# Reordering the head of a fused attention and two-layer kernel: first slot's Relu deferred, x turned earlier, x scaled by chunk

## The chip, the cores and the metric

The kernel runs on one core of a Trainium2 chip. The metric is the device time in microseconds. A core has five engines with a queue each: TensorE (PE, matrix products), VectorE (DVE), ScalarE (ACT), GpSimd (POOL) and SyncE (SP, which here issues DMA transfers).

## The reference

```
kv  = einsum('bhsd,bhse->bhde', k, v)          # B=8, H=8, S=576, D=64
o   = einsum('bhsd,bhde->bhse', q, kv)
rms = sqrt(mean(o*o, axis=-1) + 1e-6)
x   = (o / rms * g_norm), heads side by side    # 4608 x 512
h   = x @ w_in                                  # w_in 512 x 2048
g   = s * relu(h)**2 + b
out = g @ w_out                                 # w_out 2048 x 512
```

The two weights arrive as 64-bit floats; q, k, v and g_norm as 32-bit floats.

## The kernel before

**Tiling.** The 4608 rows of x are worked in 36 chunks of 128 rows, four chunks to a unit, nine units. For each chunk `attention` (or, for later units, `attention_of_two`) turns q (`turn`, `take`), multiplies it by the block-diagonal k-v product (`product`), squares and sums the rows (`square`: an ACT square and a DVE row sum), takes the root (`root`, ACT), normalises (`norm`, DVE) and turns the result so that x's features lie on partitions (`turn_x`). Turned x of a unit is one tile `xT` of 4 feature parts by 512 columns, 128 columns a chunk. Each feature part has a column of g_norm (`g_col`) that it is multiplied with.

**How x is turned and scaled in the first unit.** Chunks 0 and 1 are turned by four PE transposes each (L487); the results are scaled by g_col while they leave PSUM, chunk 0 on ACT (L490), chunk 1 on DVE (L494). Chunks 2 and 3 are turned by one DVE transpose each (L499), and once both are there `scale_x` (L507 to L510) multiplies both on ACT, in place, in four instructions of 128x256.

**The weights.** A weight tile of 1 MB is loaded by SP into one of three buffers (`w_raw`, L187) and made into 32-bit floats in four steps: `hi` (ACT, L225), `lo` (ACT, L230), `shift` (DVE, L235) and `plus` (DVE, L245). `plus` also issues the next load, into the buffer that it has just freed (`send_w`, L1246). Tiles 0 and 1, the two halves of the first two blocks of w_in, are each converted in two halves, so that the first products can begin earlier; tile 0 becomes `wa` of step 0, tile 1 `wb` of step 0. Tiles 2 to 7 are the rest of w_in, 8 to 15 are w_out.

**The first unit.** Products of the first layer are 16 slots (`mm1_plain`, L669). A slot is `block`: eight matmuls over the four feature parts (16 records in the profile) into a PSUM bank, then Relu on ACT (L682) and a square on DVE (L683). Slot 0 multiplies chunks 0 and 1 by `wa` of step 0, slot 1 the same chunks by `wb`, slot 2 chunks 2 and 3 by `wa`, slot 3 these by `wb`, and slots 4 to 15 repeat it for the next three steps. Even slots use the two x banks by turns, odd slots the two y banks. `first_unit` (L1381) puts the conversion of one tile behind most slots.

After the slots comes the second layer of the unit (`mm2`). The bias is part of it: DVE sums the rows of w_out into `b_row` (`column_sums`, L307), `bias_row` (L353) makes `b_sq` (L355) and PE multiplies the two into `b_ps`; it is called from `with_bias` (L986) after the fifth step of the second layer. Later units multiply with fewer products by sums and differences of quarters; the change does not touch them.

**Order.** The order of work on each engine is that of the program text: the kernel is scheduled by hand. The head, L1296 to L1344, is a list of calls; an instruction that waits holds everything behind it on its engine. In the head the order on ACT after chunk 0's scaling is: second half of tile 0, Relu of slot 0, square of chunk 2, first half of tile 1, square of chunk 3, second half of tile 1, both roots, the scaling of chunks 2 and 3, Relu of slot 1, tile 2.

Of the kernel before, what the change touches and what calls it, by code (L numbers as in the profile page):

```python
# [11 lines left out]
AF = mybir.ActivationFunctionType  # L12
# [4 lines left out]
def kernel(  # L17
# [39 lines left out]
    nc = tc.nc  # L57
# [8 lines left out]
    KC = DM // P  # L66
# [23 lines left out]
    def matmul(o, lhsT, rhs, start, stop):  # L90
        nc.tensor.matmul(o, lhsT=lhsT, rhs=rhs, start=start, stop=stop, skip_group_check=True)  # L91
# [246 lines left out]
    g_col = const.tile([P, KC], FP32, name="g_col")  # L338
# [63 lines left out]
    def half_of(name, c):  # L402

        if c % 2 == 0:
            two_of[name] = attp.tile([P, 2 * DM], FP32, name=name, tag=name)
        t = two_of[name]
        if name == "qT":
            return t.rearrange("p (a x) -> p a x", a=NP)[:, :, c % 2 * P : c % 2 * P + P]
        return t[:, c % 2 * DM : c % 2 * DM + DM].rearrange("p (h d) -> p h d", h=H)

    def small(name, n, i=""):
        return attp.tile([P, n], FP32, name=name, tag=f"{name}{i}")

    def attention(c):

        st = {}  # L420

        def turn():
            st["qT"] = half_of("qT", c)
            if c % 2 == 0:
                ps = ps_a.tile([P, NP, P], FP32, name="qT_ps", tag="x")
            else:
                tag, bufs = ("y", 2) if c == 1 else ("z", 1)
                ps = bank_of("q", tag, bufs).rearrange("p b (m n) -> p (b m) n", m=2)
            for p in range(NP):
                nc.tensor.transpose(ps[:, p, :], q_in[c][:, 2 * p : 2 * p + 2, :], ident)  # L430
            st["q_ps"] = ps

        def take():
            if c % 2 == 0:
                nc.vector.tensor_copy(out=st["qT"], in_=st["q_ps"])  # L435
            else:
                nc.scalar.copy(st["qT"], st["q_ps"])

        def product():
            ps = bank_of("att", "xy"[c % 2]).rearrange("p b (m n) -> p (b m) n", m=2)  # L440
            if c < 2:
                for p in range(NP):
                    matmul(ps[:, p, :], st["qT"][:, p, :], bd_kv[0][:, p, :], True, True)
            for w in range(4 if c >= 2 else 0):
                for p in range(NP):
                    nc.tensor.matmul(
                        ps[32 * p : 32 * p + 32, w, :],
                        lhsT=st["qT"][:, p, 32 * w : 32 * w + 32],
                        rhs=bd_kv[0][:, p, :],
                        start=True,  # L450
                        stop=True,
                    )
            st["x"] = ps.rearrange("p c (l d) -> p (c l) d", l=2)

        def square():
            st["xn"] = half_of("xn", c)
            nc.scalar.activation(st["xn"], st["x"], AF.Square)
            st["ss"] = small("ss", H, c % 2)
            nc.vector.reduce_sum(st["ss"], st["xn"], axis=mybir.AxisListType.X)  # L459

        def root():
            st["rms"] = small("rms", H, c % 2)
            nc.scalar.activation(st["rms"], st["ss"], AF.Sqrt, bias=eps_col, scale=1.0 / D)

        def norm():
            inv = small("inv", H, c % 2)
            nc.vector.reciprocal(inv, st["rms"])
            shape = (P, H, KC, D // KC)
            nc.vector.tensor_tensor(
                out=st["xn"].rearrange("p h d -> p (h d)").rearrange(  # L470
                    "p (c h e) -> p h c e", c=KC, h=H
                ),
                in0=st["x"].rearrange("p h (c e) -> p h c e", c=KC),
                in1=inv.unsqueeze(2).unsqueeze(3).to_broadcast(shape),
                op=ALU.mult,
            )

        def turn_x():
            u, j = divmod(c, 4)
            if j == 0:  # L480
                xT[u] = xp.tile([P, KC, 2 * TB], FP32, name="xT", tag="xT")
            to = xT[u][:, :, j * P : j * P + P]
            if c < 2:
                ps = ps_t.tile([P, KC, P], FP32, name="xT_ps", tag="t")
                xn = st["xn"].rearrange("p h d -> p (h d)")
                for i in range(KC):
                    nc.tensor.transpose(ps[:, i, :], xn[:, i * P : i * P + P], ident)  # L487
                for i in range(KC):
                    if c == 0:
                        nc.scalar.activation(  # L490
                            to[:, i], ps[:, i], AF.Copy, scale=g_col[:, i : i + 1]
                        )
                    else:
                        nc.vector.tensor_scalar(  # L494
                            out=to[:, i], in0=ps[:, i], scalar1=g_col[:, i : i + 1],
                            scalar2=None, op0=ALU.mult,
                        )
                return
            nc.vector.transpose(  # L499
                out=to, in_=st["xn"].rearrange("p h d -> p (h d)").rearrange("p (c x) -> p c x", c=KC)  # L500
            )
            if j % 2 == 1:
                scale_x(u, j - 1)

        return turn, take, product, square, root, norm, turn_x

    def scale_x(u, j):  # L507
        to = xT[u][:, :, j * P : j * P + 2 * P]
        for i in range(KC):
            nc.scalar.activation(to[:, i], to[:, i], AF.Copy, scale=g_col[:, i : i + 1])  # L510
# [134 lines left out]
    def bank_of(key, tag, bufs=2):  # L645
        bank[key] = ps_f.tile([P, 2, TB], FP32, name=f"{tag}_ps", tag=tag, bufs=bufs)
        return bank[key]
# [12 lines left out]
    def g_tile(name, s):  # L660
        if s % 2 == 0:
            g_pair[name, s // 2] = gp.tile([P, 2, 2, TB], FP32, name=name, tag=name)
        ga[name, s] = g_pair[name, s // 2][:, s % 2]
        return ga[name, s]

    def g_s1(s):
        add(ga["s1", s], ga["a21", s], ga["a22", s])

    def mm1_plain(s):  # L669


        def block(lower, half, name, tag):
            ps = bank_of("c", tag)
            w = (wb if lower else wa)[s]
            for c in range(KC):
                for b in range(2):
                    matmul(
                        ps[:, b, :], w[:, c, b], xT[0][:, c, half * TB : half * TB + TB],
                        b == 0 and c == 0, c == KC - 1,
                    )  # L680
            t = g_tile(name, s)
            nc.scalar.activation(t, ps, AF.Relu)  # L682
            nc.vector.tensor_mul(t, t, t)  # L683

        def c22():
            block(1, 1, "a22", "y")
            g_tile("s1", s)
            g_s1(s)

        return [  # L690
            lambda: block(0, 0, "a11", "x"),
            lambda: block(1, 0, "a12", "y"),
            lambda: block(0, 1, "a21", "x"),
            c22,
        ]

# [562 lines left out]
    def hi(n, h=None):  # L1259
        fold_hi(blocks[n], h)  # L1260

    def lo(n, h=None):
        round_lo(blocks[n], h)

    def shift(n, h=None):
        shift_hi(blocks[n], place(n), h)

    def plus(n, h=None):
        add_lo(blocks[n], place(n), h)
        if h != 0:  # L1270
            send_w()
# [17 lines left out]
    turn, take, product, square, root, norm, turn_x = zip(*(attention(c) for c in range(4)))  # L1289
# [3 lines left out]


    slots0 = [slot for s in range(NS) for slot in mm1_plain(s)]
    turn[0]()  # L1296
    turn[1]()
# [12 lines left out]
    norm[1]()  # L1310
    take[3]()
    hi(0, 0)
    product[2]()
    lo(0, 0)
    shift(0, 0)
    turn_x[0]()
    plus(0, 0)
    product[3]()
    hi(0, 1)
    turn_x[1]()  # L1320
    lo(0, 1)
    shift(0, 1)
    plus(0, 1)
    slots0[0]()
    square[2]()
    hi(1, 0)
    lo(1, 0)
    shift(1, 0)
    plus(1, 0)
    square[3]()  # L1330
    hi(1, 1)
    lo(1, 1)
    shift(1, 1)
    plus(1, 1)
    root[2]()
    norm[2]()
    turn_x[2]()
    root[3]()
    norm[3]()
    turn_x[3]()  # L1340
    slots0[1]()
    for step in (hi, lo, shift, plus):
        step(2)
# [37 lines left out]
    def first_unit():  # L1381
        for n, slot in enumerate(slots0):
            if n > 1:
                slot()
            if n in tile_at:
                for step in (hi, lo, shift, plus):
                    step(tile_at[n])
            if n in more_at:
                more(more_at[n])
# [166 lines left out]
```

## Time and profile before

| | |
|---|---|
| time, median of 3 | 926.41 us (925.38 to 927.22) |
| span of the profiled execution | 924.5 us |
| PE busy | 911.0 us, 99% |
| PE weight load busy | 827.1 us, 89% |
| DVE busy | 678.8 us, 73% |
| ACT busy | 209.2 us, 23% |
| GpSimd busy | 220.2 us, 24% |
| mean granted PE clock | 0.996 |
| DMA | 167.70 MB, mean 181 GB/s |

A line of the order of time gives start, duration, engine, line of the kernel, operation, output and input, shapes and count; in brackets the idle time of the engine just before, and what ended it. A line of the stretches gives the stretch, its length, and for PE, PE weight load, DVE, ACT and GpSimd the busy time and the number of instructions; then the granted clock, the DMA share and GB/s. `L91` is the helper through which nearly all matmuls go, so the names of the tiles (x_ps, y_ps, b_ps) tell products apart.

The waits of the first 80 us that are longest for PE, ACT and DVE, once the k-v product is made:

| who waited | for | us |
|---|---|---|
| DVE a L683 | ACT a L682 | 5.2 in 2, longest 2.7 |
| ACT a L682 | PE x_ps L91 | 4.9 in 3, longest 3.7 |
| ACT xT L510 | DVE xT L499 | 3.8 |
| PE y_ps L91 | DVE wb L245 | 3.3 |
| PE x_ps L446 | DVE qT L435 | 2.0 |

### The profile page before, as it was taken

How to read it: one execution, taken by the hardware profiler on the slowest of the kernel's cores; microseconds unless marked ns; L12 is line 12 of the kernel's file. 1: busy time of each engine (PE TensorE's matmuls, PEld its weight loads, DVE VectorE, ACT ScalarE, POOL GpSimd, SP SyncE). 2: the span in 40 equal slices, each digit the busy share in tenths (PEclk: the TensorE clock that was granted, in tenths of full speed). 3: DMA queues.
4: the chain of work that ended last, by engine and by line, in shares of the span. 5: the costliest groups of instructions: out<-in, count | busy, mean ns of one | idle time of the engine just before them, and what ended most of it. 6: DMA issues, size and time to landing. Idle time of an engine off the chain costs nothing.

```text
span 924.5 us, 18300 instructions
## 1 busy us (share of the span) xinstructions
PE 911.0 (99%) x7272; PEld 827.1 (89%) x7272; DVE 678.8 (73%) x1149; ACT 209.2 (23%) x382; POOL 220.2 (24%) x412
## 2 busy tenths in 40 slices
PE   7899999999999999999999999999999999999998
PEld 7688888888888998899889988999889988998898
DVE  2679869587667975887678867786678768864685
ACT  2666122310124002310232013301340033002200
POOL 2000005203623232630264034603330200020000
PEclk9899999999999999999999999999999999999999
DMA  9486957429931894179425954387418900890085
GB/s 270 136 300 234 282 145 222 112 68 325 333 105 35 262 335 126 26 220 308 146 81 157 296 180 115 96 295 247 116 42 278 296 12 12 257 310 26 12 251 183
DMA packets 113605, 167.70 MB, mean 181 GB/s; under 512 B 28400, under 2 KB 45552, under 8 KB 113520
## 3 DMA queue, kind: packets, MB, share of 16 engines
q1 hardware_dynamic: 95504, 141.98, 49.0%
q0 software_dynamic: 14560, 22.31, 8.3%
q10 hardware_dynamic: 3456, 2.23, 0.9%
q8 instruction: 58, 0.95, 0.4%
q14 instruction: 27, 0.22, 0.1%
HBM read 142.35 MB, written 24.12 MB: 180 GB/s over the span
## 4 chain that ended last, share of the span: by engine, by line
PE 97%; DVE 1%; DMA 1%; issue 0%; SPq 0%; ACT 0%; DVEq 0%
PE x_ps L91 51%; PE y_ps L91 29%; PE z_ps L91 11%; PE kv_ps L380 2%; PE y_ps L559 2%; DMA kv_sb<-in_v_dram 1%; PE qT_ps L548 0%; SPq L107 0%; DVE o L858 0%; DVE ss L459 0%; DVE sub L253 0%; DVE qT L435 0%; DVE xn L592 0%; DVE a L253 0%; PE xT_ps L487 0%
## 5 line engine op out<-in xcount | busy, mean ns | idle before, releaser
L1376 POOL DMA_DIRECT2D q_sb<-in_q_dram x256 | 143.7, 569 | 150.4 <-issue 120.0
L703 ACT COPY r<-x_ps 128x512 f32<-128x512 f32 x96 | 55.9, 583 | 453.8 <-PE x_ps L91 424.0
L967 POOL DMA_DIRECT2D out_dram<-o x110 | 54.8, 505 | 406.3 <-DVE o L858 277.7
L91 PE MATMUL x_ps<-w_sb,sub 128*128 128x128 f32 x1176 | 149.3, 276 | 0.7 <-DVE r L858 0.7
L91 PEld LDWEIGHTS x_ps<-w_sb,sub 128*128 128x128 f32 x1176 | 139.7, 192 | 1.5 <-DVE r L858 0.9
L91 PE MATMUL x_ps<-xs,ws 128*128 128x256 f32 x512 | 122.3, 382 | 0.0
L91 PE MATMUL y_ps<-xs,wb 128*128 128x256 f32 x512 | 121.8, 380 | 0.2 <-issue 0.2
L91 PEld LDWEIGHTS x_ps<-xs,ws 128*128 128x128 f32 x512 | 96.2, 190 | 16.5 <-issue 3.8
L91 PEld LDWEIGHTS y_ps<-xs,wb 128*128 128x128 f32 x512 | 96.7, 190 | 14.2 <-issue 0.6
L250 DVE TENSOR_TENSOR a<-y_ps,r 128x512 f32<-128x512 f32 x64 | 44.1, 689 | 83.6 <-ACT r L703 73.3
L91 PE MATMUL x_ps<-xT,wa 128*128 128x256 f32 x384 | 89.6, 380 | 0.5 <-DVE xT L494 0.5
L91 PEld LDWEIGHTS x_ps<-xT,wa 128*128 128x128 f32 x384 | 72.3, 190 | 10.5 <-ACT w_raw L225 0.7
L91 PE MATMUL x_ps<-w_sb,a 128*128 128x128 f32 (+1 forms) x432 | 64.9, 298 | 0.0
L91 PE MATMUL y_ps<-w_sb,a 128*128 128x128 f32 (+1 forms) x416 | 62.1, 295 | 0.0
L91 PEld LDWEIGHTS x_ps<-w_sb,a 128*128 128x128 f32 x432 | 59.0, 191 | 3.2 <-issue 0.4
L91 PE MATMUL x_ps<-xT,ws 128*128 128x256 f32 x256 | 61.2, 382 | 0.0
L91 PE MATMUL z_ps<-xT,wa 128*128 128x256 f32 x256 | 60.5, 379 | 0.0
L658 DVE SCALAR_TENSOR_TENSOR a<-a 128x512 f32<-128x512 f32 x82 | 56.7, 692 | 2.8
L91 PEld LDWEIGHTS y_ps<-w_sb,a 128*128 128x128 f32 x416 | 56.1, 192 | 2.1
L91 PEld LDWEIGHTS z_ps<-xT,wa 128*128 128x128 f32 x256 | 48.6, 190 | 6.6
L91 PEld LDWEIGHTS x_ps<-xT,ws 128*128 128x128 f32 x256 | 48.1, 190 | 6.5
L858 DVE SCALAR_TENSOR_TENSOR r<-x_ps,s_col,o 128x256 f32<-128x256 f32 (+1 forms) x84 | 34.7, 413 | 25.7 <-PE x_ps L91 24.1
(157 smaller groups left out, 1268.8 us busy)
## 6 DMA issues: line engine op xcount, KB each, us to landing
w_sb<-w SPq DMA_DIRECT2D x343, 256.0 KB, 4.7
w_raw<-in_moe_w_in_dram SPq DMA_DIRECT2D x8, 1024.0 KB, 7.7
w_raw<-in_moe_w_out_dram SPq DMA_DIRECT2D x8, 1024.0 KB, 5.2
w_sb<-w SPq DMA_DIRECT2D x14, 512.0 KB, 9.0
w<-sub POOLq DMA_DIRECT2D x28, 256.0 KB, 6.3
w_sb<-in_k_dram SPq DMA_DIRECT2D x24, 288.0 KB, 5.1
w_sb<-in_v_dram SPq DMA_DIRECT2D x24, 288.0 KB, 5.1
out_dram<-o POOLq DMA_DIRECT2D x92, 64.0 KB, 3.6
```

Of the source, the lines that this page charges most:

```text
L91: nc.tensor.matmul(o, lhsT=lhsT, rhs=rhs, start=start, stop=stop, skip_group_check=True)
L250: nc.vector.tensor_tensor(out=o, in0=a, in1=b, op=ALU.add)
L380: nc.tensor.matmul(ps[r][(r ^ l) * HB : (r ^ l) * HB + HB, i, :], lhsT=kv[l][0][rows, j, :], rhs=kv[l][1][rows, j, :], start=(j == 0), sto ...
L559: nc.tensor.matmul(ps[l][32 * p : 32 * p + 32, r, lo:hi], lhsT=bd_kv[b % 2][rows, p, at : at + 32], rhs=st["qT"][rows, p, lo:hi], start=Tr ...
L658: nc.vector.scalar_tensor_tensor(t, t, 0.0, t, ALU.max, ALU.mult)
L703: nc.scalar.copy(st[name], src)
L858: nc.vector.scalar_tensor_tensor(o, ps, s_col, other, ALU.mult, ALU.add)
L967: queues[s % 2].dma_start(out=view[b, jj, :, cols], in_=st[name, j][s * w : s * w + w, cols])
L1376: load()
```

## The change

Three things are done to the head, for the same end: to let the first slots of PE follow each other with less waiting.

- `block` no longer issues Relu and square itself but returns them as a function. For slot 0 that function is called at the end of the head, after the second weight tile's conversion and the work on chunks 2 and 3; everywhere else it is called at once.
- Chunks 0 and 1 are turned ahead of the q products of chunks 2 and 3 (`turn_x[0]` before `product[2]`, `turn_x[1]` before `product[3]`), and the squares, roots and norms of chunks 2 and 3 are moved between the steps of tile 1's conversion.
- Chunks 2 and 3 are scaled each by itself, as soon as it is turned: in eight ACT instructions of 128x128 instead of four of 128x256. Later units still use `scale_x`.

```diff
--- before.py
+++ after.py
@@ -499,8 +499,8 @@
             nc.vector.transpose(
                 out=to, in_=st["xn"].rearrange("p h d -> p (h d)").rearrange("p (c x) -> p c x", c=KC)
             )
-            if j % 2 == 1:
-                scale_x(u, j - 1)
+            for i in range(KC):
+                nc.scalar.activation(to[:, i], to[:, i], AF.Copy, scale=g_col[:, i : i + 1])
 
         return turn, take, product, square, root, norm, turn_x
 
@@ -678,19 +678,22 @@
                         ps[:, b, :], w[:, c, b], xT[0][:, c, half * TB : half * TB + TB],
                         b == 0 and c == 0, c == KC - 1,
                     )
-            t = g_tile(name, s)
-            nc.scalar.activation(t, ps, AF.Relu)
-            nc.vector.tensor_mul(t, t, t)
+            def out_of():
+                t = g_tile(name, s)
+                nc.scalar.activation(t, ps, AF.Relu)
+                nc.vector.tensor_mul(t, t, t)
+
+            return out_of
 
         def c22():
-            block(1, 1, "a22", "y")
+            block(1, 1, "a22", "y")()
             g_tile("s1", s)
             g_s1(s)
 
         return [
             lambda: block(0, 0, "a11", "x"),
-            lambda: block(1, 0, "a12", "y"),
-            lambda: block(0, 1, "a21", "x"),
+            lambda: block(1, 0, "a12", "y")(),
+            lambda: block(0, 1, "a21", "x")(),
             c22,
         ]
 
@@ -1310,34 +1313,35 @@
     norm[1]()
     take[3]()
     hi(0, 0)
+    lo(0, 0)
+    turn_x[0]()
     product[2]()
-    lo(0, 0)
     shift(0, 0)
-    turn_x[0]()
     plus(0, 0)
+    turn_x[1]()
     product[3]()
     hi(0, 1)
-    turn_x[1]()
     lo(0, 1)
     shift(0, 1)
     plus(0, 1)
-    slots0[0]()
+    out_of_first = slots0[0]()
     square[2]()
+    square[3]()
     hi(1, 0)
     lo(1, 0)
     shift(1, 0)
+    root[2]()
+    root[3]()
     plus(1, 0)
-    square[3]()
+    norm[2]()
     hi(1, 1)
     lo(1, 1)
     shift(1, 1)
+    turn_x[2]()
     plus(1, 1)
-    root[2]()
-    norm[2]()
-    turn_x[2]()
-    root[3]()
     norm[3]()
     turn_x[3]()
+    out_of_first()
     slots0[1]()
     for step in (hi, lo, shift, plus):
         step(2)
@@ -1381,7 +1385,9 @@
     def first_unit():
         for n, slot in enumerate(slots0):
             if n > 1:
-                slot()
+                out_of = slot()
+                if out_of:
+                    out_of()
             if n in tile_at:
                 for step in (hi, lo, shift, plus):
                     step(tile_at[n])
```

## The prediction

> **What bounds the kernel now.** I read the 40 slices first, for where TensorE (PE) is not saturated.
>
> ```profile
> ## 2 busy tenths in 40 slices
> PE   7899999999999999999999999999999999999998
> DVE  2679869587667975887678867786678768864685
> PEclk9899999999999999999999999999999999999999
> ```
>
> PE is under 90% only in the first two slices (46 us) and the last; the second also has a granted clock of 0.8. So only the head can give time, or something that begins in the head and pushes on. I then read that head by the waits, by stretches of 2 us, and in order of time. The stretches (PE, weight load, VectorE (DVE), ScalarE (ACT), GpSimd; then clock, DMA share, GB/s):
>
> ```profile
> 28.00:30.00 2.00, 0.38 (x2) 0.00 (x0) 0.96 (x2) 1.59 (x4) 0.00 (x0) 1.00 0.89 234
> 30.00:32.00 2.00, 0.36 (x1) 0.39 (x2) 1.86 (x4) 2.00 (x5) 0.00 (x0) 0.67 0.70 271
> 32.00:34.00 2.00, 2.00 (x6) 1.53 (x6) 1.83 (x5) 0.58 (x3) 0.00 (x0) 0.50 0.00 0
> 36.00:38.00 2.00, 2.00 (x7) 1.62 (x6) 0.39 (x1) 1.58 (x4) 0.00 (x0) 0.62 0.95 347
> ```
>
> PE pauses from 28.4 to 31.64 and then runs at half clock; from 0.67 and 0.62 in the border stretches, half clock lasts from 30.7 to 37.5. The order of time says why it pauses:
>
> ```profile
> 24.54 3.84 PE L91 MATMUL x_ps<-xT,wa 128*128 128x256 f32 x16 [0.54 <-DVE xT L494]
> 28.41 0.60 ACT L682 ACTIVATE a<-x_ps 128x512 f32<-128x512 f32 x1 [3.74 <-PE x_ps L91]
> 31.64 6.58 PE L91 MATMUL y_ps<-xT,wb 128*128 128x256 f32 x16 [3.26 <-DVE wb L245]
> 36.42 1.70 ACT L510 ACTIVATE xT<-xT,g_col 128x256 f32<-128x256 f32 x4 [3.85 <-DVE xT L499]
> 38.06 3.62 PE L91 MATMUL x_ps<-xT,wa 128*128 128x256 f32 x16
> ```
>
> Call a group of 16 records of line 91 a slot: slot 0 at 24.54, slot 1 at 31.64, slot 2 at 38.06. ACT stands 3.74 us at slot 0's Relu, with the next weight tile's folding and the squares of chunks 2 and 3 queued behind it; so slot 1 waits for its weights. Slot 2 takes chunks 2 and 3 of x, whose scaling ACT begins only at 36.42. From 38.06 on slots follow at 3.45 us.
>
> A second thing nearly binds, 60 us later:
>
> ```profile
> 63.65 1.14 ACT L225 ACTIVATE w_raw<-w_raw 128x1024 f32<-128x1024 f32 x1 [1.83 <-DMA w_raw<-in_moe_w_out_dram]
> 64.82 0.69 DVE L235 TENSOR_SCALAR w_up<-w_raw 128x1024 uint32<-128x1024 uint32 x1 [0.90 <-ACT w_raw L225]
> 103.30 0.28 DVE L355 TENSOR_SCALAR b_sq<-b_sq,b_col 128x128 f32<-128x128 f32 x1
> 103.67 1.09 PE L91 MATMUL b_ps<-b_row,b_sq 128*128 128x512 f32 x2
> ```
>
> After the 0.38 us at 65.89 the order of time shows no DVE wait until 105.42: DVE is full from 64.82 to 103.58, and PE's bias product at 103.67 starts 0.09 us after it. The DVE chain has no slack to give PE, and it starts from a load that ACT had waited for.
>
> **What the Trainium skill says.** "TensorE: Matmul & The Clock Gate", Part 1: after about 3.4 us of idling, watched in windows of 3,413 ns that run free of the kernel, the array drops to half clock and needs a busy window to return. The trace agrees: 30.7 to 37.5 is 6.8 us, two windows, after one (27.3 to 30.7) with 1.1 us of work. The same page, "Architectural detail": ACT and DVE queues are strict FIFO. Agrees: the fold at 29.38 stood behind the Relu. "ScalarE: Activation LUTs", "What ACT_TABLE_LOAD costs": 186 ns + 0.833 ns an element, 93 ns for a pointer operand, 93 ns overlap with the next. For the 128x256 scale that is 492 ns; the trace has 1.70 us for four, 0.49 each with a 0.40 step.
>
> **The change, part by part.** I place each instruction with the steps of the trace: ACT 128x512 0.55 (weights) or 0.48 (square, Relu); DVE 0.42 for a half-tile shift, 0.69 for 128x512, about 0.08 of overlap between independent operations, none between dependent ones.
>
> *Turning chunk 0 and 1 first.* norm[0] ends at 20.08, so chunk 0's transposes run 20.15 to 20.8, in PE time that was idle (2.04 us before the product at 20.74); product[2] keeps its place (qT is ready at 20.69), chunk 1's transposes run at 21.8 instead of 23.34, product[3] at 22.35. ACT scales chunk 0 from 21.0 (was 22.44); DVE scales chunk 1 from 22.6 (was 24.04), right after the first half tile's add. The second half's shift and add then end at 24.9 (were 26.3). Slot 0 begins when product[3] leaves PE, 23.4, and ends at 26.9: 1.2 earlier. Nothing is added; four transposes change places.
>
> *Relu and square of slot 0 deferred.* ACT goes straight on: squares of chunk 2 at 23.1 and 3 at 23.6, then the fold of weight tile 1 at 24.1 (was 29.38). That tile was issued at 13.7 and landed 10.3 us later, at 24.0, so this just fits. DVE: two row sums 24.8 to 26.1, shift 26.0, add 26.6 to 27.3 (was 31.50); slot 1 starts at 27.35. Then norm[2] to 28.1, second shift, turn of chunk 2 to 29.1, add 29.0 to 29.7, norm[3] to 30.6, turn of chunk 3 to 31.3 (was 36.38). Slot 1's second half thus waits from 29.1 to 29.8 and ends at 31.55. The deferred pair runs after the last scale; bank and tile of slot 0 are next wanted by slot 4, at 38.6, so I cost it at nothing for PE, but 0.49 on ACT before tile 2's fold.
>
> *Clock.* PE's pauses are then 0.5 and 0.7 us. The worst 3.41 us window (26.9 to 30.3) is about 65% busy; in the trace of before the window 17.0 to 20.4 is about 50% busy and the clock stayed 1.00. I take full clock: slot 1 needs 3.45 us and not 6.58.
>
> *Scale by chunk.* Eight 128x128 instead of four 128x256. No row shows it from SBUF; lower end: the PSUM row of line 490, 1.14 for four; upper end: no cheaper than a 128x256, 1.70. The skill's price gives 386 ns and a 0.29 step, 1.27 for four (an estimate); I take that. Chunk 2's four lie in 29.1 to 30.4, beside DVE. Chunk 3's run 31.34 to 32.6; slot 2 needs only the first (0.29 steps against 0.86 us of matmul per part), so it starts at 31.7. Against 38.06 PE leads by 6.4 us.
>
> *What that releases.* On ACT: chunk 3's scales let the next instruction in at 32.5, Relu of slot 0, of slot 1 (32.99), and tile 2's fold at 33.5, against 38.75: 5.2 us earlier. Slot 4 needs tile 2 at 38.6; it is added by 37.0, slack 1.6 (was 2.8). From here each load is issued when a tile's add frees one of three buffers (42.2, 44.3, 47.3 before), the DMA share is 0.86 to 1.02 from 44 to 56, and ACT waits for the landings. Nothing but the start moves, so the whole train, to the load at 63.65 and the full DVE stretch behind it, comes 5.2 earlier: b_sq ends at 98.4. PE would be at the bias product at 97.3. A wait of 6.4 - 5.2 - 0.1 = 1.1 us appears there, and 5.2 us stay. Queued behind it on PE is only PE's own work, which was its bound anyway. Later waits of PE sum to 0.9 us, all short, and later loads hang on PE's progress, so the lead carries to the end: 926.4 - 5.2 = 921.2.
>
> **Rivals.** (A) As above: 921.2. (B) The loads go with PE's lead, since the landings are quicker than in the trace or DVE has slack I don't see: 926.4 - 6.4 = 920.0. For it: DMA is idle from 39 to 43. Against: no DVE wait is listed in 66 to 103. (C) The free-running window catches slot 1's two pauses and halves the clock: 6.8 us at half cost up to 3.4 us, PE's lead is 3.0: 923.4. Against: the 50% window above. (D) The lead is lost later, at loads I take for relative ones: about 926.2. For it: DMA share of 0.57 after 92 us; against: no PE wait for a DMA after the head. (E) Slower: the fold of tile 1, now at 24.1, meets a landing that slips by 4 us (the first loads share a DMA share of 1.0 with q); all of ACT behind it waits, PE pauses over a window and loses 3.4 at half clock, with 0.5 for the longer scaling: 6.4 - 4 - 3.4 - 0.5 = -1.5, 927.9. Against: that landing is unmoved by the change.
>
> **How the numbers follow.** A 0.60, B 0.12, C 0.13, D 0.08, E 0.07. Faster: A, B, C and hardly more, 0.86; same 0.07; slower 0.07. Range: B's 920.0 less 0.4 for scale steps at the lower end gives 919.6; C's 923.4 plus half of the 1.8 us by which the times before spread gives 924.3.
>
> **What would show it.** Right: no wait of ACT at slot 0's Relu, clock 1.00 throughout, slot 1 at about 27.4, slot 2 at about 31.7, tile 2's fold at about 33.5, b_ps waiting about 1.1 us for b_sq at about 98.4. Wrong: a clock of 0.5 near 30; ACT's fold of tile 1 waiting for a DMA; the load at 63.65 moving by less than 5; a new wait of PE after 105.

## The result, and the profile after

The changed kernel took 920.22 us, median of 6 executions (919.90 to 920.73), against 926.79 us for the kernel before on the same chip, also 6. The ratio is 0.9931, with a 95% interval of 0.9919 to 0.9944: 6.4 us less, between 5.2 and 7.5. The forecast was 921.2.

The slices of the changed kernel's page, for PE, DVE and the granted clock:

```profile
PE   7999999999999999999999999999999999999998
DVE  2789777687577985887677867787678768864685
PEclk9999999999999999999999999999999999999999
```

The second slice has gone from 8 to 9 on PE and the dent in the clock from 8 to 9; PE's share is the same from there on. The stretches around the former pause (stretch, length, PE, weight load, DVE, ACT, GpSimd, then clock, DMA share, GB/s):

```profile
26.00:28.00 2.00, 1.73 (x9) 1.23 (x8) 1.83 (x5) 1.65 (x5) 0.00 (x0) 1.00 0.73 146
28.00:30.00 2.00, 1.69 (x9) 1.16 (x7) 1.95 (x5) 0.70 (x3) 0.00 (x0) 1.00 1.00 355
30.00:32.00 2.00, 1.91 (x9) 1.35 (x9) 1.40 (x2) 1.05 (x4) 0.00 (x0) 1.00 0.41 99
32.00:34.00 2.00, 2.00 (x9) 1.79 (x10) 0.68 (x2) 2.00 (x6) 0.00 (x0) 1.00 0.93 309
```

Where PE stood still and then ran at 0.5, it is now over 80% busy at 1.00. In order of time:

```profile
23.63 3.72 PE L91 MATMUL x_ps<-xT,wa 128*128 128x256 f32 x16
24.74 0.73 ACT L225 ACTIVATE w_raw<-w_raw 128x512 f32<-128x512 f32 x1
27.62 1.97 PE L91 MATMUL y_ps<-xT,wb 128*128 128x256 f32 x8 [0.27 <-DVE inv L467]
29.89 1.99 PE L91 MATMUL y_ps<-xT,wb 128*128 128x256 f32 x8 [0.31 <-DVE wb L245]
31.53 1.28 ACT L503 ACTIVATE xT<-xT,g_col 128x128 f32<-128x128 f32 x4 [0.95 <-DVE xT L499]
31.98 3.72 PE L91 MATMUL x_ps<-xT,wa 128*128 128x256 f32 x16
33.67 1.14 ACT L225 ACTIVATE w_raw<-w_raw 128x1024 f32<-128x1024 f32 x1
...
56.95 1.17 ACT L225 ACTIVATE w_raw<-w_raw 128x1024 f32<-128x1024 f32 x1
...
97.30 0.28 DVE L355 TENSOR_SCALAR b_sq<-b_sq,b_col 128x128 f32<-128x128 f32 x1
...
97.70 1.06 PE L91 MATMUL b_ps<-b_row,b_sq 128*128 128x512 f32 x2
```

Slot 1 now comes in two halves, each waiting 0.3 us for DVE; tile 1's fold (its conversion, seen here by the first step `hi`) starts at 24.74 instead of 29.38, slot 2 at 31.98 instead of 38.06, tile 2's fold at 33.67 instead of 38.75, and the bias product at 97.70 instead of 103.67. Span against span is 924.5 - 918.1 = 6.4 us: 6.0 of it is there at the bias product and stays the same up to 653 us; another 0.4 appears there because the trace of before has a short pause of PE at 654 us that no engine ends (listed as "issue", 0.2). The second trace of before, below, has it too (653.96), but those of turn_alone, chunk_alone and before_warm, in which the work there is the same, have not; so it is not put down to the change, and its cause stays open.

Everything up to tile 2's fold is as forecast. Two lines are not: tile 9's fold at 56.95 (63.65 before) waits for no load and is 6.7 us earlier, not 5.2, and the bias product finds b_sq ready. The experiments were chosen for these two, and for what each part of the change brings.

### The profile page after: what moved, and what is told of

The parts are those of the page before. It is cut to its first block, busy times and chain, and to the rows that moved or that the text cites. A ratio compares the mean times of both kernels' runs of the same rounds, so it can differ in the third digit from the quotient of the medians.

```text
span 918.1 us, 18306 instructions
## 1 busy us (share of the span) xinstructions
PE 907.6 (99%) x7272; PEld 824.6 (90%) x7272; DVE 678.2 (74%) x1149; ACT 210.3 (23%) x386; POOL 220.2 (24%) x412
## 4 chain that ended last, share of the span: by engine, by line
PE 96%; DVE 2%; DMA 1%; ACT 0%; issue 0%; SPq 0%; DVEq 0%
PE x_ps L91 51%; PE y_ps L91 29%; PE z_ps L91 11%; PE kv_ps L380 2%; PE y_ps L559 2%; DMA kv_sb<-in_v_dram 1%; PE qT_ps L548 0%; DVE xn L469 0%; SPq L107 0%; DVE ss L459 0%; DVE o L861 0%; DVE sub L253 0%; DVE wb L245 0%; DVE xn L592 0%; DVE a L253 0%
```

## The experiments

Each was timed beside the kernel before, whose medians on the chips used lay between 925.92 and 927.20 us. Ratios are to it, with their 95% intervals.

**The kernel before once more.**

> The kernel before, once more, for a second trace of it. Theory (the load at 63.65 waits 1.8 us by chance of DMA sharing): tile 9's fold moves by about 1 us from 63.65 in this trace while tile 2's fold stays at 38.7, and b_sq at 103.3 moves with it. Rival (the order of the loads fixes it): both stay within 0.2 us. The half clock near 31 to 37 us shows again if it is the pause of 3.3 us that causes it, whatever the phase of the window; if the phase decides, it may start elsewhere or be one window long.

Measured: 926.96 us, ratio 1.0008 (1.0000 to 1.0016). Its trace:

```profile
32.16 3.69 PE L91 MATMUL y_ps<-xT,wb 128*128 128x256 f32 x16 [3.27 <-DVE wb L245]
37.50 3.72 PE L91 MATMUL x_ps<-xT,wa 128*128 128x256 f32 x16 [1.66 <-ACT xT L510]
61.18 1.20 ACT L225 ACTIVATE w_raw<-w_raw 128x1024 f32<-128x1024 f32 x1
101.58 0.28 DVE L355 TENSOR_SCALAR b_sq<-b_sq,b_col 128x128 f32<-128x128 f32 x1
104.90 0.43 DVE L253 TENSOR_TENSOR b<-b_row 128x256 f32<-128x256 f32 x1 [3.04 <-ACT b_row L358]
103.22 1.02 PE L91 MATMUL b_ps<-b_row,b_sq 128*128 128x512 f32 x2
```

The same kernel, and two things that I had read as its nature are gone. Tile 9's fold came at 61.18 with no wait for its load (63.65 in the first trace), so b_sq was done 1.4 us ahead of PE. Tile 9's load landed 4.8 us after its issue here and 7.7 us in the first trace: the "no slack" of that trace was a late landing in one execution. And slot 1 ran its 3.69 us at full clock behind the same pause of 3.27 us. Then slot 2 waits 1.66 us for chunk 2's and 3's scaling instead: what half clock lost, it had mostly lost where PE would have waited. From the start of slot 0 to that of slot 2 it is 12.45 us here and 13.52 in the first trace, so two windows at half clock cost 1.1 us and not the 2.9 by which slot 1 was longer.

The second trace also allows a comparison across all the runs. In every kept trace, of both kernels and of all experiments, the bias product starts 65.6 to 65.7 us after slot 2, and the execution ends 820.3 to 820.9 us after the bias product, although b_sq is ready 0.1 us ahead of PE in one trace and over 2 us in others. Whatever these kernels differ by is made before slot 2 starts.

**Slot 0's Relu and square alone put off.**

```diff
-    slots0[0]()
+    out_of_first = slots0[0]()
...
     turn_x[3]()
+    out_of_first()
     slots0[1]()
```

> Only slot 0's Relu and square are put off to the end of the head; the other orders of before stay. Theory of two limits (end set by the later of PE's lead and the train of loads and DVE work): slot 1 follows slot 0 without a pause, clock 1.00, slot 2 at about 33.5 (PE lead 4.5), tile 2's fold at about 35.6 (train lead 3.2): time 3 to 4 us below before. Rival (PE pause and half clock are the whole gain): 6 us below, as the full change. Rival (turn order is the main part): under 1.5 us below.

Measured: 923.73 us, ratio 0.9969 (0.9958 to 0.9979), 2.9 us less: just under what I expected. In its trace slot 1 follows slot 0 without a wait and slot 2, which waits 1.7 us for x, starts at 35.74, but the clock was at half from 23 to 26.4, at the chunk products and turns ahead of slot 0, a place that neither trace of before had shown.

**The turn order alone.**

```diff
+    turn_x[0]()
     product[2]()
...
+    turn_x[1]()
     product[3]()
```

> Only the PE transposes of chunks 0 and 1 go ahead of the products of chunks 2 and 3. Theory: slot 0 starts at about 23.4 instead of 24.5, all behind it comes 1.2 earlier, pause and half clock stay: time 1.0 to 1.3 us below before. Rival (hidden by the pause anyway): 0.0.

Measured: 924.37 us, ratio 0.9979 (0.9972 to 0.9985), 1.9 us less: more than expected. Slot 0 starts at 23.93; a pause of 3.27 us and a half clock of one window (30.4 to 33.8) stay behind it, and slot 2 waits only 0.3 us. What the surplus over 1.3 is stands with the table of clocks below.

**Scale by chunk alone.**

```diff
-            if j % 2 == 1:
-                scale_x(u, j - 1)
+            for i in range(KC):
+                nc.scalar.activation(to[:, i], to[:, i], AF.Copy, scale=g_col[:, i : i + 1])
```

> Only the scaling of chunks 2 and 3 by chunk, eight 128x128 instead of four 128x256. Theory: chunk 2's four run at about 35 beside DVE's norm of chunk 3, chunk 3's four take 1.3 us from 36.4; but slot 1 at half clock ends at about 38 and both slot 2 and the Relu of slot 1 wait for it: 0.0 to 0.3 us below before. Rival (scaling is what slot 2 waits for): 0.5 us below.

Measured: 927.82 us, ratio 1.0022 (1.0014 to 1.0030), 1.5 us more by the medians: slower, which neither reading expected. Its trace on ACT and DVE:

```profile
36.72 1.28 ACT L503 ACTIVATE xT<-xT,g_col 128x128 f32<-128x128 f32 x4 [2.49 <-DVE xT L499]
37.91 0.29 ACT L463 ACTIVATE rms<-ss,eps_col 128x8 f32<-128x8 f32 x1
38.23 0.20 DVE L467 RECIPROCAL inv<-rms 128x8 f32<-128x8 f32 x1 [1.54 <-ACT rms L463]
```

In the old order of calls the root of chunk 3 comes after the turn of chunk 2. With the scale inside the turn, ACT waits 2.49 us for chunk 2's transpose, scales, and only then takes chunk 3's root, for which DVE waits 1.54 us. Slot 2 starts 14.01 us after slot 0, against 12.45 in the second trace of before: 1.6 us later. The full change calls both roots first and so escapes it.

**The changed kernel less one part: Relu back in place; old turn order; scaling by pairs.** The edit shown is the first; the other two take back the edits of the turn order and of the scaling shown above.

```diff
-    out_of_first = slots0[0]()
+    slots0[0]()()
...
-    out_of_first()
```

> The changed kernel with slot 0's Relu and square back in their place behind slot 0; the rest of the change stays. Theory: ACT stands at the Relu until 27, tile 1's fold goes to about 28.6, slot 1 to about 31, with a pause over 3 us and half clock behind it; slot 2 at 36 to 37, tile 2's fold at 36.5 to 37.5: time 4 to 5 us above the changed kernel, 1.5 to 2.5 below before. Rival (the turns and the scaling carry half of the gain): 3 us above the changed kernel or less.

Measured: 924.58 us, ratio 0.9986 (0.9980 to 0.9993): 4.4 us above the changed kernel, as expected. Its trace has the pause back (3.86 us) and half clock from 29.8 to 36.6, two windows; all 21 executions have a mean clock of 0.998 or 0.996, so the 4.4 is the deferral with the half clock that it prevents.

> The changed kernel with the products of chunks 2 and 3 again ahead of the turns of chunks 0 and 1. Theory: slot 0 at about 24.6, DVE and ACT behind it 1.2 later: time 1.0 to 1.3 us above the changed kernel. Rival (PE's order in the head is hidden by DVE's work): under 0.3.

Measured: 922.33 us, ratio 0.9957 (0.9945 to 0.9970): 2.1 us above, again more than the 1.3 of the order. Its trace gives a candidate:

```profile
18.00:20.00 2.00, 1.07 (x10) 0.83 (x9) 1.68 (x4) 1.20 (x4) 0.00 (x0) 1.00 1.05 360
20.00:22.00 2.00, 0.89 (x32) 0.81 (x32) 1.97 (x5) 1.61 (x3) 0.00 (x0) 1.00 1.05 385
22.00:24.00 2.00, 2.00 (x36) 1.58 (x32) 0.92 (x2) 1.13 (x5) 0.00 (x0) 0.65 1.01 382
24.00:26.00 2.00, 1.74 (x20) 0.94 (x12) 0.22 (x1) 1.30 (x4) 0.00 (x0) 0.50 0.25 94
```

About 1 us of PE work in each 2 us from 18 to 22, and then half clock from 22.6 on for one window.

> The changed kernel with chunks 2 and 3 scaled together in four 128x256. Theory: slot 2 needs only the first of four, 0.1 us later than by chunk, and tile 2's fold comes 0.4 later: time 0.1 to 0.4 us above the changed kernel. Rival (scale by chunk carries 1 us or more): 1 us above.

Measured: 920.23 us, ratio 0.9935 (0.9922 to 0.9947): no difference from the changed kernel. Slot 2 waits 0.2 us for the first of four 128x256 and starts 0.1 us later after the first q product than in the changed kernel, as worked out; whether that reaches the end these medians can't tell.

**Filling PE's pause in the kernel before**, without and with DVE relieved ahead of the bias product. The relief, not shown, moves `sub_w_out(6, 3, 5)` behind the bias product.

```diff
     slots0[0]()
+    warm(11)
     square[2]()
```

> The kernel before with eleven matmuls of the identity (into a bank that nothing reads) between slot 0 and slot 1, which fill PE's pause without delaying slot 1. Theory of two limits: clock 1.00, slot 1 ends at about 35, slot 2 at about 36.9 (1.2 earlier), but the train of loads and DVE work is as before, so PE waits at the bias product: time 0.0 to 0.4 us below before. Rival (half clock is what the change saves): 1.2 to 3.1 us below.

Measured: 926.82 us, ratio 1.0003 (0.9995 to 1.0011).

> As the kernel before with the eleven filling matmuls, and besides four DVE subtractions (2.5 us, w_out's column 3 less column 5, not needed until the third group of products behind) moved from before the bias product to behind it. Theory of two limits: the bias product no longer waits for DVE, PE keeps its 1.2 us: time 1.0 to 1.3 us below before. Rival (the train is no limit): the same as without the move.

Measured: 927.22 us, ratio 1.0003 (0.9995 to 1.0011). The first alone would have spoken for the limit on DVE. The second refutes it: with DVE freed there is still no gain. Its trace says why:

```profile
28.86 2.62 PE L91 MATMUL warm_ps<-ident 128*128 128x128 f32 x22
32.19 3.75 PE L91 MATMUL y_ps<-xT,wb 128*128 128x256 f32 x16 [0.71 <-DVE wb L245]
37.62 3.72 PE L91 MATMUL x_ps<-xT,wa 128*128 128x256 f32 x16 [1.68 <-ACT xT L512]
```

Slot 1 at full clock ends early, and slot 2 waits 1.68 us for the scaling of x on ACT, which hangs on DVE's work in the head and not on PE's clock. The filling did not keep the clock whole in every execution: 10 of the 13 without relief and 9 of the 14 with it have a mean clock of 0.998 or less, and the trace of the first (before_warm) is at half clock from 22.6 to 26.0, ahead of slot 0. But the executions at 1.000 took 925.26 (2) and 925.95 (5), within 0.4 us of the kernel before at 1.000 (925.64, below). The half clock behind the pause is a consequence that costs 1.1 us; the late x of chunks 2 and 3 is the greater cost.

**DVE ahead of the bias product, relieved and loaded, in the changed kernel.** The edit shown is the load; the relief is the same move as above.

```diff
                     sub_w_out(6, 3, 5)
+                    sub_w_out(6, 3, 5, [0, 1])
```

> The changed kernel with the same four DVE subtractions moved behind the bias product. Theory: in the changed kernel's trace PE and DVE reach the bias product within 0.1 us of each other, so freeing DVE alone gains 0.0 to 0.2 us. Rival (DVE still holds PE's lead back): 0.5 us or more below the changed kernel.

Measured: 920.43 us, ratio 0.9931 (0.9917 to 0.9945): nothing.

> The changed kernel with two of those four DVE subtractions done twice (same result), 1.2 to 1.3 us more on DVE before the bias product. Theory: DVE has 0.1 us of slack there, so the time is 1.1 to 1.3 us above the changed kernel and PE shows a wait at b_ps. Rival (PE alone sets the end, DVE runs beside it): 0.0.

Measured: 920.55 us, ratio 0.9936 (0.9921 to 0.9950): 0.3 us above the changed kernel, within both intervals; 1.1 to 1.3 was expected. Its trace:

```profile
93.71 3.69 DVE L253 TENSOR_TENSOR w_t<-w_dn,w_up 128x512 f32<-128x512 f32 x6
97.32 0.28 DVE L355 TENSOR_SCALAR b_sq<-b_sq,b_col 128x128 f32<-128x128 f32 x1
98.12 1.02 PE L91 MATMUL b_ps<-b_row,b_sq 128*128 128x512 f32 x2
```

Six subtractions instead of four, and b_sq is still done 0.5 us before PE comes. PE has no wait from 60 to 120 us. So DVE is no limit of the changed kernel.

**The pause ahead of the chunk products filled, in the changed kernel with the old turn order.** This asks whether half clock in the head is the surplus of the turn order over 1.3.

```diff
     turn[3]()
+    fill = ps_t.tile([P, DM], FP32, name="fill_ps", tag="t")
+    for _ in range(7):
+        matmul(fill[:, :P], ident, ident, True, True)
     root[0]()
```

> The changed kernel with the old turn order (products of chunks 2 and 3 ahead of the turns of chunks 0 and 1), and seven matmuls of the identity, which nothing reads, in PE's pause of 2 us ahead of those products. The same without them took 922.33 us, 2.1 above the changed kernel, and its trace ran at half clock from 22.2 to 26. Theory (of the 2.1, the order itself is about 1.3, the rest is half clock that the 2 us pause lets in, in some executions): no half clock, 921.3 to 921.7 us. Rival (the order itself costs 2.1): 922.2 to 922.5 us.

Measured: 921.59 us, ratio 0.9947 (0.9933 to 0.9961). The trace has full clock throughout:

```profile
19.17 1.73 PE L91 MATMUL fill_ps<-ident 128*128 128x128 f32 x14
21.38 1.08 PE L446 MATMUL x_ps<-bd_kv,qT 128*32 128x128 f32 x32 [0.48 <-DVE qT L435]
25.18 3.84 PE L91 MATMUL x_ps<-xT,wa 128*128 128x256 f32 x16 [0.54 <-DVE xT L494]
33.76 3.72 PE L91 MATMUL x_ps<-xT,wa 128*128 128x256 f32 x16
```

The median lies where the theory put it, 1.4 above the changed kernel and 0.7 below the unfilled one; the intervals of the two ratios overlap. In the traces one window does cost that much there: from the first q product, at 16.18 and 16.44, to slot 0 it is 10.10 us unfilled and 8.74 filled, as in both traces of before. But that is no explanation of the medians. Of the five unfilled executions four have a mean clock of 1.000, and these took 922.17 in the median. That the 0.7 is half clock is not shown; it may be chance, with five executions on each side.

**The clock of each execution.** Every execution has a mean granted clock: one window of 3.4 us at half (22.6 to 26.0 in the trace of after_old_turn, not the 22.2 of the expectation above) takes 0.5 x 3.4 / 924 = 0.002 off it. The 106 executions of the kernel before, taken beside the experiments, sort by it:

| mean clock | executions of before | median us | lowest, highest |
|---|---|---|---|
| 1.000 | 39 | 925.64 | 925.10, 926.48 |
| 0.998 | 34 | 926.49 | 924.99, 927.95 |
| 0.996 | 19 | 926.57 | 925.98, 927.30 |
| 0.994 | 14 | 927.99 | 927.71, 928.53 |

Of the changed kernel's 6 all are at 0.999 or 1.000. At 1.000 the turn order alone took 924.41 (6 executions) and the deferral alone 922.23 (3): 1.2 and 3.4 us below 925.64, as worked out for both. The deferral's other five, at 0.997 to 0.999, took 923.66 to 924.56, so its median is high by half clock. The turn order's eleven at 0.998 took 924.33, no more than its six at 1.000. Its median is therefore 1.2 us of order, and 0.7 that the kernel before loses to half clock in the median (926.32 against 925.64) and it doesn't.

## Why the prediction was right, and where it was not

*The head.* Right, instruction by instruction. Slot 0 at 23.63 (forecast 23.4), tile 1's fold 24.74 (24.1), slot 1 27.62 and 29.89 (27.35 and 29.8), slot 2 31.98 (31.7), tile 2's fold 33.67 (33.5). The whole head of that execution is 0.24 us late, so the steps are closer than they look. Taking single parts out bears out their sizes: 4.4 us for the deferral, 1.4 for the order of the turns in the trace without half clock. Singly, deferral and turn order bring 3.4 + 1.2 = 4.6 of 5.2 at full clock. Deferral alone leaves the old places of squares, roots and norms; that the rest is theirs was not tried by itself. One count of the prediction is off without effect: eight transposes change places, four for each of the two chunks.

*Scale by chunk.* The price was right: 1.28 us for four, forecast 1.27, an estimate from the price that the Trainium skill gives for an activation ("ScalarE: Activation LUTs", "What ACT_TABLE_LOAD costs"). It buys nothing at the end that the medians show, and without the move of the roots it costs 1.5 us.

*Clock.* Full clock was right, but the argument for it was weak. I took one window about 50% busy, in one trace, for proof that such a window is safe. Other kernels with that turn order dropped to half right there in the execution that was traced: in before_warm, defer_alone, after_old_turn and chunk_alone the 3.41 us (a window, as long as each stretch at half) ahead of the drop hold 1.36, 1.48, 1.49 and 1.51 us of PE work. My window held 1.64, and was followed by none. The emptiest 3.41 us of the changed kernel's trace at that place hold 1.87, since chunk 0's transposes now lie in the gap; none of the six traces with the new turn order drops there. So full clock was luck in part: I looked for its danger at slot 1, where the pauses are short, and the gap ahead of the q products, which the changed turn order happened to narrow, was the nearer one. In "TensorE: Matmul & The Clock Gate", Part 1, the Trainium skill says that the windows run free of the kernel; it follows that one trace shows one phase, and the mean clocks in the table above, 1.000 to 0.994, are those of the same kernel with none, one, two and three windows lost. The changed kernel is also steadier: its 6 executions spread over 0.8 us, the 106 of before over 3.5.

*What that releases.* This step failed: "Nothing but the start moves, so the whole train, to the load at 63.65 and the full DVE stretch behind it, comes 5.2 earlier". The start did move by that (tile 2's fold 5.1, the issue of tile 9 from 55.9 to 50.5), but the train came 6.0 earlier at b_sq, since tile 9 landed 6.3 us after its issue and not 7.7. And DVE was no limit: the second trace of before has b_sq 1.4 us ahead of PE, relief brought nothing in either kernel, and 1.2 us more of DVE work brought no wait. I had taken a coincidence of 0.09 us in one trace for a bound; there too the bias product came 65.6 us after slot 2, as everywhere. The wait of 1.1 us for b_sq never came. (The table of the longest waits ahead of the prediction lacks ACT's waits for weight loads, 6.0 us in 4; the one for tile 9 is one of them.) The term of the sum is then PE's own lead: forecast 6.4, measured 6.1 at slot 2 and 6.0 at the bias product. The course of things was rival B's (920.0), to which I gave 0.12.

*What PE's lead is made of.* Against executions of before at full clock the gain is 5.2 us (925.64 to the 920.46 of the three at 1.000), and so it is in the traces: from the first q product to slot 2 it is 21.19 us in the second trace of before and 15.95 in the changed kernel. The median gains more because 67 of the 106 executions of before lost something to half clock. The forecast's 6.4 was reckoned against a trace with two such windows. They make 1.1 us of it, not the 3.1 by which slot 1 was slower, for most of these were covered by the wait for x, as the second trace and the fillings show. That the gain at full clock equals the forecast's 5.2 is chance: the forecast came to it as 6.4 less the wait for b_sq.

## What to carry to other kernels

On an engine that works in program order, move the instruction that waits for the longest job behind the work that feeds the next job: here one Relu and its square held up a weight tile, two squares and through them x, for 4.4 us with the half clock that followed. Before a near-coincidence of two chains goes into a sum as a limit, look at it in a second execution, or load the chain by a known amount. And an edit that puts a waiting instruction into a helper must be checked for what stands behind it at each place of call: the same eight scalings cost 1.5 us or nothing.

## What the runs showed of the hardware that I had not expected

Half clock appeared behind a PE pause of 2.0 us with sparse work around it (the stretches from 18 to 22 us above are 45 to 55% busy), not only behind the pause of 3.3 us, and not in every execution of either. Where it fell decided its price: 1.4 us ahead of slot 0, next to nothing on slot 1 of the turn order alone. The landing of one and the same 1 MB load (tile 9) came 7.7 us after its issue in the first trace of before, 4.8 in the second and 6.3 in the changed kernel's, with the loads issued in the same order; b_sq then had 0.1, 1.4 and 0.1 us to spare, and the end moved by nothing for it.
